# Filter transposed in 16 bits, other first loads, an uneven last tile, and a new fixed order, in a kernel of a long convolution beside a token-mixing MLP

## The chip, the cores and the metric

The kernel runs on one core of a Trainium2 chip. The time is the device time of one execution in microseconds; the median of three runs before the change is 177.09 us (176.99 to 177.10). A core has five engines that each work through a queue of their own in order: TensorE (PE, the matmuls; PEld is its weight load), VectorE (DVE), ScalarE (ACT), GpSimd (POOL) and SyncE (SP, which here only starts transfers). TensorE writes into PSUM, from which another engine has to move every result into the main on-chip memory (an *evacuation*).

## What is computed

```python
x = A_q                                                # 2048 tokens x 640 channels, bf16
g = sigmoid((x * gate_w).sum(-1, keepdims=True))
# a: a gated long convolution
k_shift[t] = sum_j A_k[t - 3 + j] * shift_k[j]         # four taps, causal
kv = k_shift * A_v
y  = irfft(rfft(kv, 4096) * rfft(ssm_k, 4096))[:2048]  # one filter of 2048 taps for each channel
a  = q * (y + kv * ssm_D)
# b: a MLP that mixes tokens
h  = layernorm(x)                                      # over the 640 channels
u  = gelu(einsum("bsd,sf->bdf", h, w1) + b1)           # 2048 tokens -> 1536
b  = transpose(einsum("bdf,fs->bds", u, w2) + b2)      # 1536 -> 2048 tokens
out = g * a + (1 - g) * b
```

## The kernel before

Everything is matmuls on 128x128 blocks. The Fourier transforms are products with cosine and sine tables: FE and FN, which are made on the chip with a sine on ScalarE, and FO, which is loaded. The program writes the whole computation as 649 operations (a matmul group, a step on another engine, or a transfer), each with a number. Three strings fix what runs when:

- `_ORDER` (L1318) lists the numbers. Each engine's queue, SP's queue of transfers included, gets its operations in this order.
- `_SLOTS` gives each matmul group one of four PSUM slots (128 x 1024 in f32, two banks each). A group waits until its slot has been evacuated.
- `_ENG` says for the operations that either engine can do ("A" ScalarE, "D" VectorE) which one does: the evacuations of the filter part, the normalizations of the layer norm, and the permutations of k.

Waits follow from the regions that operations read and write (class `_Tracker`; its `mm`, L286 to L309, issues every matmul, at L298; every ScalarE step of a general kind is at L600, VectorE's and POOL's elementwise steps at L556 and L570, and the evacuations at L615 for ScalarE and L616 for VectorE).

The parts that the change touches:

- *Filter.* `ssm` holds the filters, five blocks `db` of 128 channels, in two halves `h` of 1024 taps. `transp(h, db)` (L798) transposes one half of one block with eight matmuls against the identity (group "wtr") and evacuates the slot, 128 x 1024, to `wT` with a factor 1/1024. For h = 0 a POOL step first adds the skip term D, which lies in `dcol`, to the first tap; `dcol` is an evacuation of the transposed small rows `rows` (group "cst"). `wblock(h, db)` (L818) multiplies `wT` with the tables in two groups of 16 matmuls ("W") and evacuates each ("Wb"). Ten transpositions, 80 matmuls; twenty W groups, 320 matmuls.
- *k and kv.* POOL forms four `KF`, the short convolution's taps on diagonals, from `cw` (L971). A tile of k is permuted (`k_turn`, L702, "kperm"), transposed by a transfer into KT, and multiplied with KF on TensorE; the product with v is transformed.
- *Layer norm.* `ln_tile` (statistics, VectorE), `ln_scale` (POOL) and `ln_apply` ("nrm", either engine), for 16 rows of 640.
- *MLP.* The first product in groups of eight matmuls of 320 columns, with the Gelu as evacuation into GT; ScalarE has to load another function table between the sine and the first Gelu. b1 goes through a transposition of its own (`consts`, L791) into `cc`. The second product (L1108 to L1125) takes the 640 columns of a tile as 320 + 320 in two banks. The last tile (hk = 3) has its two halves one after the other, so that the first half is complete early.
- *End.* The inverse transforms, and for each tile the combination with g. In the last tile two VectorE steps ("fin", `last_stt`, L624), one for each column half, take PSUM and the convolution's part together, and one store of 160 KB follows.

In the order before, SP starts its first loads as: the X tile 2, filter block 1, the first half of block 0, block 2, FO in two parts, X3, b1, block 3, X1, three quarters of X0, k, block 4, k, the last quarter of X0, the second half of block 0, w1. TensorE begins with dummy matmuls on zeros (`zz`), a pair of which stands later between two transpositions. POOL adds D to block 1 and block 0, then to block 2, then makes two KF, and so on. ScalarE's table load for the Gelu comes just before the first Gelu.

Of the kernel before, what the change touches and what calls it, by code (L numbers as in the profile page):

```python
# [19 lines left out]
class _Tracker:  # L20
# [265 lines left out]
    def mm(self, ps_ap, lhsT, rhs, start, stop, final_val, inc, transpose=False):  # L286
        acc_r = []
        for a in (lhsT, rhs):
            for r in self.regions(a):
                acc_r.append((r, "R"))  # L290
        acc = list(acc_r)
        ps_regs = self.regions(ps_ap)
        if start:
            for r in ps_regs:
                acc.append((r, "W"))
        need = self.deps_for("PE", acc)
        self.do_waits("PE", need)
        ins = self.nc.tensor.matmul(ps_ap, lhsT=lhsT, rhs=rhs, start=start, stop=stop, skip_group_check=True)  # L298
        src = ("eng", "PE", final_val)
        for reg, mode in acc_r:  # L300
            self.add_record(reg, "R", src)
        for r in ps_regs:
            self.add_record(r, "W", src)
        if inc:
            ins.then_inc(self.clk["PE"], 1)
            self.cnt["PE"] += 1
            assert self.cnt["PE"] == final_val, (self.cnt["PE"], final_val)
            self.hist["PE"].append(dict(self.known["PE"]))
        return ins  # L309
# [123 lines left out]
def _build(nc, A_q, A_k, A_v, A_shift_k, A_ssm_k, A_ssm_D, B_x, B_w1, B_b1, B_w2, B_b2, gate_w, out):  # L433
# [10 lines left out]
    with ExitStack() as es:  # L444
# [190 lines left out]
        def memset(eng, ap, val, prio=None):  # L635
            return nolock(eng, 0.2, lambda s: T.op(eng, lambda e: e.memset(ap, val), [], [ap]), [], [ap], prio=prio)

        def mms(vt, items, prio=None, name="mm"):
            dur = sum(max(n_of(r) / 2400.0 + 0.0025, 0.056) for _, _, r, _, _ in items)
            rd = []  # L640
            for _, l, r, _, _ in items:
                rd += [l, r]

            def emit(s):
                fv = T.cnt["PE"] + 1
                for k_, (o, l, r, st, sp) in enumerate(items):
                    T.mm(o(s), l, r, st, sp, fv, k_ == len(items) - 1)
            return SC.add("PE", dur, emit, rd, [], prio=prio, vt=vt, name=name)

        ndma = [0]  # L650
# [16 lines left out]
        def dr(t, off, ap):  # L667
            return bass.AP(tensor=t.tensor, offset=t.offset + off, ap=ap)
# [10 lines left out]
        def ssm_load(h, a, b):  # L679
            dma(ssm[:, a:b, 1024 * h:1024 * h + 1024], dr(A_ssm_k, 128 * S * a + 1024 * h, [[S, 128], [128 * S, b - a], [1, 1024]]), 128 * (b - a) * 2048, chain=True, rate=({0: 262.0, 1: 223.0}.get(a, RL3)) if h == 0 else 385.0)  # L680
# [9 lines left out]
        def qrow(hk):  # L690
            return row8(A_q, hk) if hk >= 2 else dr(A_q, 512 * hk * D, [[4 * D, 128], [1, 4 * D]])

        def x_load(hk):
            dma(X[:, hk, :, :], qrow(hk), 128 * 5120, chain=True, rate=(352.0 if hk == 0 else 415.0))

# [24 lines left out]

        small(rows[0:ND, 0, 128:256], dr(A_ssm_D, 0, [[128, ND], [1, 128]]), 1280, "QA")
        small(rows[0:20, 0, 0:128], dr(A_shift_k, 0, [[128, 20], [1, 128]]), 5120, "QA")
        ssm_load(0, 0, 1)
        for a, b in ((0, 1), (1, 4)):
            dma(X[:, 0, a:b, :], dr(A_q, a * D, [[4 * D, 128], [1, (b - a) * D]]), 128 * 1280 * (b - a), chain=True)
        ssm_load(1, 0, 1)
        for db in range(1, ND):
            dma(ssm[:, db, :], dr(A_ssm_k, 128 * S * db, [[S, 128], [1, S]]), 128 * 4096, chain=True)
        for p in range(2):
            dma(FO[:, p, :, :, :, :].rearrange("q a b c d -> q (a b c d)"), dr(odd_tab, 1024 * p, [[2048, 128], [1, 1024]]), 128 * 2048, chain=True)  # L730
        for hk in range(1, 4):
            x_load(hk)
        small(bt[:, 0:8].rearrange("q (a b) -> q a b", a=2), dr(B_b2, 0, [[4, 128], [512, 2], [1, 4]]), 2048, "SP", chain=True)
        small(bt[:, 8:16], dr(B_b2, 1024, [[8, 128], [1, 8]]), 2048, "SP", chain=True)
# [63 lines left out]
        def transp(h, db):  # L798
            vt = _VT("cv")
            items = []  # L800
            if h == 0:
                w0 = V(ssm, db * S, [[1, 1]])
                tt("POOL", w0, w0, dcol[:, db:db + 1], ALU.add)
            for j in range(7, -1, -1):
                items.append(((lambda s, j=j: s[:, 128 * j:128 * j + 128]), V(ssm, db * S + 1024 * h + j, [[8, 128]]), ident[:, :], True, True))
            m_ = mms(vt, items, name="wtr")
            evac("wT", V(wT, 2 * h * SL + 128 * db, [[SL, 2], [D, 4], [1, 128]]), (lambda s: s[:, :].rearrange("q (a b c) -> q a b c", a=2, b=4)), vt, 1.0 / 1024.0)

        def table(p, kt, c, k2):
            if p % 2:  # L810
# [291 lines left out]
        def w2t(hk, p, ft):  # L1102
            if hk < 2:
                return V(W2, (W2S[hk][ft // 4] + ft % 4) * 512 + p, [[4, 128]])
            return V(W2, W2P[ft] * 512 + 4 * (hk - 2) + p, [[8, 128]])

        INVP = ((0, 2, 1, 3), (1, 3, 0, 2))
        for hk, p in [(hk, p) for hk in range(2) for p in range(4)] + [(hk, p) for p in INVP[1] for hk in (2, 3)]:  # L1108
            for a in {(1, 0): (4, 6, 8), (2, INVP[1][0]): (10,)}.get((hk, p), ()):
# [6 lines left out]
            for a in range(na):  # L1116
                items = []
                for ft, ci in order[a * (24 // na):(a + 1) * (24 // na)]:
                    items.append((chk(ci), w2t(hk, p, ft), GT[:, ft, 320 * ci:320 * ci + 320], ft == 0, ft == FT - 1))
                mms(vt, items, name="m2")  # L1120
                if last_:
                    vt.keep = True
                    lastvt.append(vt)
# [111 lines left out]
        def inverse(h, Z, G=None):  # L1235
            for p in INVP[h]:
# [25 lines left out]
                if h == 1 and p == INVP[1][-1]:  # L1262
# [2 lines left out]
                    t = 12 + p  # L1265
                    ts("DVE", cg[:, 1, :], cg[:, 1, :], c2[:, t:t + 1], None, ALU.add, mode=2)
                    for ci in range(2):
                        last_stt(O1[:, 3, p, 320 * ci:320 * ci + 320], chk(ci), omg[:, t:t + 1], cg[:, 1, 320 * ci:320 * ci + 320], lastvt[ci])
                    dma(rows_of(1, p, 1, 1), O1[:, 3, p, :], 128 * 1280, sem="out")
                elif h == 0:  # L1270
                    dma(ov, qv, 128 * 2560, stream="POOL", prio=0, accum=True)
                    dma(rows_of(0, p, 0, 2), ov, 256 * 1280, sem="out")
# [43 lines left out]


_ORDER = """  # L1318
# [22 lines left out]
"""  # L1341
_ENG = "DAAAAADDAAAAAADDDDDAAADDDADDDDADDAAAAAAAAAAAAAAADD"
_SLOTS = "1120021323201331122022011133001030332021001010110220110131230121002123231321103301332230032032101133201012203121332133113300113"
# [1 line left out]
_INS = ['A_q', 'A_k', 'A_v', 'A_shift_k', 'A_ssm_k', 'A_ssm_D', 'B_x', 'B_w1', 'B_b1', 'B_w2', 'B_b2', 'gate_w']  # L1345
_OUTS = [((1, 2048, 640), 'bfloat16')]
# [23 lines left out]
```

## Time and profile before

| | before |
|---|---|
| median of 3 runs | 177.09 us (176.99 to 177.10) |
| profiled execution | 177.12 us, of which the span from the first to the last instruction is 175.1 us |
| granted TensorE clock | 1.00 throughout |
| TensorE busy | 170.0 us (97%) |
| VectorE busy | 168.9 us (96%) |
| ScalarE busy | 107.6 us (61%) |
| POOL busy | 42.7 us (24%) |
| data moved | 44.06 MB in 33248 packets, mean 252 GB/s |

The busy time of each engine over five stretches (us, busy time, number of instructions, granted clock, share of the transfer engines, GB/s):

```profile
core 0: us, PE busy (x) PEld busy (x) DVE busy (x) ACT busy (x) POOL busy (x), PEclk, DMA share, GB/s
0.00:6.60 6.60, 5.25 (x20) 1.78 (x21) 4.73 (x19) 2.79 (x4) 1.62 (x12) 1.00 0.73 227
6.60:30.30 23.70, 23.70 (x404) 23.40 (x405) 23.45 (x62) 22.56 (x26) 17.80 (x31) 1.00 1.09 332
30.30:44.30 14.00, 13.48 (x152) 10.32 (x149) 13.87 (x14) 12.69 (x16) 0.00 (x0) 1.00 1.10 326
44.30:171.90 127.60, 127.59 (x988) 102.72 (x988) 125.80 (x94) 69.56 (x116) 23.24 (x19) 1.00 0.93 230
171.90:175.10 3.20, 0.00 (x0) 0.00 (x0) 1.01 (x2) 0.00 (x0) 0.00 (x0) 1.00 0.76 266
```

The first stretch ends with the first transposition of the filter; the second holds the whole filter part; the third the k part and the first half of the MLP's first product up to the first Gelu; the fourth everything else up to the last matmul; the fifth the closing steps and the last store. A row of the timeline is start, length, engine, line, instruction, output <- inputs with shapes, and in brackets the idle time ahead of it with what ended it. Matmuls are pipelined, and the end that a row gives is modelled.

### The profile page before, as it was taken

The page shows a single profiled execution, that of the slowest core. Times are in us where ns is not written, and L with a number is a line of the kernel's source. Part 1 is how long each engine was busy: PE and PEld are TensorE (multiplying, and loading weights), DVE is VectorE, ACT ScalarE, POOL GpSimd, SP SyncE. Part 2 cuts the span into 40 slices and gives each one's busy share as a digit, 9 for nine tenths or more (in the row PEclk, how much of TensorE's full clock was granted, in tenths as well). Part 3 has the DMA queues.
Part 4 walks back from the last instruction along what each step waited for, and adds up shares of the span by engine and source line. Part 5 has one row for each costly group of instructions (what it writes and reads, how often), then busy time and mean ns, then how long its engine had stood idle before and what let it go on. Part 6 is the DMA issues. An engine that isn't in the chain of part 4 may idle for free.

```text
span 175.1 us, 3683 instructions
## 1 busy us (share of the span) xinstructions
PE 170.0 (97%) x1559; PEld 138.2 (79%) x1559; DVE 168.9 (96%) x187; ACT 107.6 (61%) x160; POOL 42.7 (24%) x62
## 2 busy tenths in 40 slices
PE   7999999999899999999999999999999999999992
PEld 2599999877697767777777778888899998698782
DVE  7899999999999999999999999999999999999984
ACT  4499999997999997877556214222215105645760
POOL 3199891000000650003202202220055000052200
PEclk9999999999999999999999999999999999999999
DMA  5999999999999799992999999999939999549598
GB/s 144 397 421 405 376 200 225 380 375 221 179 383 356 172 192 192 186 358 57 178 174 365 353 211 349 282 207 240 300 108 187 197 177 372 241 65 209 106 233 292
DMA packets 33248, 44.06 MB, mean 252 GB/s; under 512 B 12112, under 2 KB 24656, under 8 KB 33104
## 3 DMA queue, kind: packets, MB, share of 16 engines
q1 hardware_dynamic: 28024, 32.68, 57.6%
q0 software_dynamic: 5168, 11.14, 37.4%
q8 instruction: 12, 0.20, 0.4%
q14 instruction: 4, 0.03, 0.1%
q10 hardware_dynamic: 40, 0.01, 0.0%
HBM read 27.44 MB, written 2.62 MB: 172 GB/s over the span
## 4 chain that ended last, share of the span: by engine, by line
PE 93%; DMA 3%; ACT 2%; DVE 0%; DVEq 0%; SPq 0%; issue 0%
PE pp L298 93%; DMA ssm<-in_A_ssm_k_dram 3%; ACT L600 1%; ACT ksh L600 1%; ACT GT L600 0%; DVE O L627 0%; DVEq L426 0%; SPq L272 0%
## 5 line engine op out<-in xcount | busy, mean ns | idle before, releaser
L298 PE MATMUL pp<-X,ring 128*128 128x320 bf16 x384 | 55.4, 299 | 0.5 <-ACT GT L600 0.5
L556 DVE TENSOR_TENSOR C<-C 128x2560 bf16<-128x2560 bf16 (+2 forms) x38 | 54.6, 1485 | 0.3 <-ACT C L600 0.2
L298 PE MATMUL pp<-GT,W 128*128 128x320 bf16 x384 | 53.6, 299 | 0.0
L298 PEld LDWEIGHTS pp<-GT,W 128*128 128x128 bf16 x384 | 48.0, 129 | 4.6
L298 PEld LDWEIGHTS pp<-X,ring 128*128 128x128 bf16 x384 | 37.0, 98 | 15.0 <-ACT GT L600 0.8
L600 ACT ACTIVATE O<-pp,c,omg 128x640 bf16<-128x640 f32 x15 | 12.9, 883 | 24.8 <-PE pp L298 24.8
L267 POOL DMA_DIRECT2D C<-C x8 | 10.5, 1674 | 51.1 <-DVE C L556 30.0
L600 ACT ACTIVATE C<-pp 128x640 bf16<-128x640 f32 x32 | 20.4, 711 | 2.0 <-PE pp L298 2.0
L600 ACT ACTIVATE cgb<-pp,gg 128x640 bf16<-128x640 f32 x16 | 12.1, 795 | 13.3 <-PE pp L298 7.6
L615 ACT ACTIVATE C<-pp 128x1024 bf16<-128x1024 f32 x18 | 17.1, 1051 | 0.3 <-PE pp L298 0.3
L600 ACT ACTIVATE gq<-gq 128x640 bf16<-128x640 bf16 x16 | 11.6, 727 | 5.7 <-DVE gq L556 5.7
L556 DVE TENSOR_TENSOR tm<-C,C 128x5120 bf16<-128x5120 bf16 x5 | 14.1, 2819 | 0.1
L897 DVE BATCH_NORM_STATS2 stats<-X 128x6 f32<-128x320 bf16 x32 | 13.1, 470 | 0.4 <-DMA X<-in_A_q_dram 0.2
L298 PE MATMUL pp<-wT,FO 128*128 128x128 bf16 x160 | 12.4, 219 | 0.0
L600 ACT ACTIVATE GT<-pp,cc 128x640 bf16<-128x640 f32 x12 | 9.3, 793 | 4.8 <-PE pp L298 4.7
L298 PE MATMUL pp<-C,GTB 128*128 128x320 bf16 x80 | 11.9, 299 | 0.0
L298 PE MATMUL pp<-wT,FE 128*128 128x128 bf16 x120 | 11.7, 219 | 0.0
L556 DVE TENSOR_TENSOR SS<-C 128x2560 bf16<-128x2560 bf16 x8 | 11.7, 1482 | 0.0
L267 POOL DMA_DIRECT2D O<-q_hi x4 | 4.8, 1324 | 27.7 <-DVE q_hi L556 27.7
L600 ACT ACTIVATE ksh<-pp 128x1024 bf16<-128x1024 f32 (+1 forms) x12 | 10.1, 908 | 1.4 <-PE pp L298 1.3
L267 POOL DMA_DIRECT2D C<-q_hi x4 | 4.8, 1198 | 23.8 <-DVE q_hi L556 10.9
L556 DVE TENSOR_TENSOR C<-tm 128x2560 bf16<-128x2560 bf16 x7 | 10.3, 1487 | 0.1
(92 smaller groups left out, 225.3 us busy)
## 6 DMA issues: line engine op xcount, KB each, us to landing
ring<-in_B_w_dram SPq DMA_DIRECT2D x12, 512.0 KB, 8.8
W<-in_B_w_dram SPq DMA_DIRECT2D x12, 512.0 KB, 6.8
C<-C POOLq DMA_DIRECT2D x8, 640.0 KB, 8.8
kn<-in_A_k_dram SPq DMA_DIRECT2D x4, 640.0 KB, 9.6
C<-q_hi POOLq DMA_DIRECT2D x4, 640.0 KB, 9.7
out_dram<-O SPq DMA_DIRECT2D x7, 320.0 KB, 3.2
ssm<-in_A_ssm_k_dram SPq DMA_DIRECT2D x4, 512.0 KB, 7.0
X<-in_A_q_dram SPq DMA_DIRECT2D x3, 640.0 KB, 7.3
```

What stands on the lines that cost most here:

```text
L267: ins = engobj.dma_start(out_ap, in_ap, accum_op=ALU.add, max_dma_last_dim=2560)
L298: ins = self.nc.tensor.matmul(ps_ap, lhsT=lhsT, rhs=rhs, start=start, stop=stop, skip_group_check=True)
L556: o_ = SC.add(eng, d, lambda s: T.op(eng, lambda e: e.tensor_tensor(o, a, b, op), rd, [o]), rd, [o], prio=prio, name="tt")
L600: return T.op("ACT", lambda e: e.activation(o, src, func, **kw), rr + [src], ww)
L615: return either(name, o, i, [], lambda e, src: e.activation(o, src, ACT.Copy, **kw), lambda e, src: e.tensor_copy(o, src) if scale == 1.0 ...
L897: ops.append(SC.add("DVE", 0.38, (lambda o, i: lambda s: T.op("DVE", lambda e: e.bn_stats(o, i), [i], [o]))(o, i), [i], [o]))
```

## The change

1. `mm` passes its flag `transpose` on. The filter's transpositions are issued as transpositions proper, which write 16-bit results into PSUM: a group then fills half a slot, one bank in place of two, and its evacuation reads 128 x 1024 of bf16 in place of f32.
2. `_ENG`: four of the ten evacuations to `wT` are VectorE's (block 3's first half; the second halves of blocks 2, 3 and 4), in place of two others (the first halves of blocks 0 and 2). Two "Wb" evacuations go from VectorE to ScalarE. Of the 16 normalizations VectorE does 12 in place of 11. One more permutation of k (tile 2) goes to ScalarE: VectorE keeps three.
3. Loads: block 1 of the filter comes in two halves, and block 0 whole. X tile 2 comes as one quarter and three quarters (`xpart`), and X0 whole.
4. The last tile of the MLP's second product takes its columns as 512 + 128. The two closing steps have these widths, and each has a store of its own (128 KB and 32 KB). That makes 650 operations.
5. `_ORDER` and `_SLOTS` are new. The first loads go out as: X3, b1, block 2, block 1 in halves, X2 in two pieces, block 0, FO in two parts, X0, block 4, X1, k, block 3, k, w1. ScalarE's table load for the Gelu comes right after the sine, ahead of `dcol`, `cc` and `cw`. b1 is transposed ahead of the filter. TensorE transposes block 2 (second half), block 1 (first half), block 2 (first half), then after a pair of dummies block 1 (second half), and W groups follow. POOL adds D to blocks 2 and 1, makes three KF, and then adds D to block 0. At the end, the closing step of the 128 columns and its store come before that of the 512.

```diff
-        ins = self.nc.tensor.matmul(ps_ap, lhsT=lhsT, rhs=rhs, start=start, stop=stop, skip_group_check=True)
+        ins = self.nc.tensor.matmul(ps_ap, lhsT=lhsT, rhs=rhs, start=start, stop=stop, skip_group_check=True, **({"is_transpose": True} if transpose else {}))
...
-        def mms(vt, items, prio=None, name="mm"):
+        def mms(vt, items, prio=None, name="mm", transpose=False):
...
-                    T.mm(o(s), l, r, st, sp, fv, k_ == len(items) - 1)
+                    T.mm(o(s), l, r, st, sp, fv, k_ == len(items) - 1, transpose)
...
+        def xpart(hk, a, b):
+            t = qrow(hk)
+            return bass.AP(tensor=t.tensor, offset=t.offset + a * D, ap=[list(t.ap[0]), [1, (b - a) * D]])
...
-        ssm_load(0, 0, 1)
+        ssm_load(0, 1, 2)
         for a, b in ((0, 1), (1, 4)):
-            dma(X[:, 0, a:b, :], dr(A_q, a * D, [[4 * D, 128], [1, (b - a) * D]]), 128 * 1280 * (b - a), chain=True)
-        ssm_load(1, 0, 1)
-        for db in range(1, ND):
+            dma(X[:, 2, a:b, :], xpart(2, a, b), 128 * 1280 * (b - a), chain=True)
+        ssm_load(1, 1, 2)
+        for db in [d for d in range(ND) if d != 1]:
...
-        for hk in range(1, 4):
+        for hk in [k for k in range(4) if k != 2]:
...
-                items.append(((lambda s, j=j: s[:, 128 * j:128 * j + 128]), V(ssm, db * S + 1024 * h + j, [[8, 128]]), ident[:, :], True, True))
-            m_ = mms(vt, items, name="wtr")
-            evac("wT", V(wT, 2 * h * SL + 128 * db, [[SL, 2], [D, 4], [1, 128]]), (lambda s: s[:, :].rearrange("q (a b c) -> q a b c", a=2, b=4)), vt, 1.0 / 1024.0)
+                items.append(((lambda s, j=j: s[:, 64 * j:64 * j + 64].bitcast(BF16)), V(ssm, db * S + 1024 * h + j, [[8, 128]]), ident[:, :], True, True))
+            m_ = mms(vt, items, name="wtr", transpose=True)
+            evac("wT", V(wT, 2 * h * SL + 128 * db, [[SL, 2], [D, 4], [1, 128]]), (lambda s: s[:, 0:512].bitcast(BF16).rearrange("q (a b c) -> q a b c", a=2, b=4)), vt, 1.0 / 1024.0)
...
+        LASTC = (0, 512, 640)
...
-                    items.append((chk(ci), w2t(hk, p, ft), GT[:, ft, 320 * ci:320 * ci + 320], ft == 0, ft == FT - 1))
+                    c0, c1 = LASTC[ci:ci + 2] if last_ else (320 * ci, 320 * ci + 320)
+                    items.append(((lambda s, ci=ci, n=c1 - c0: s[:, 512 * ci:512 * ci + n]), w2t(hk, p, ft), GT[:, ft, c0:c1], ft == 0, ft == FT - 1))
...
-                        last_stt(O1[:, 3, p, 320 * ci:320 * ci + 320], chk(ci), omg[:, t:t + 1], cg[:, 1, 320 * ci:320 * ci + 320], lastvt[ci])
-                    dma(rows_of(1, p, 1, 1), O1[:, 3, p, :], 128 * 1280, sem="out")
+                        c0, c1 = LASTC[ci:ci + 2]
+                        last_stt(O1[:, 3, p, c0:c1], (lambda s, ci=ci, n=c1 - c0: s[:, 512 * ci:512 * ci + n]), omg[:, t:t + 1], cg[:, 1, c0:c1], lastvt[ci])
+                        o_ = rows_of(1, p, 1, 1)
+                        dma(bass.AP(tensor=o_.tensor, offset=o_.offset + c0, ap=[list(o_.ap[0]), [1, c1 - c0]]), O1[:, 3, p, c0:c1], 128 * 2 * (c1 - c0), sem="out")
...
 (_ORDER, _ENG and _SLOTS: all three strings are new)
```

More of the change, by code (lines that the diff above doesn't have):

```diff
@@ L1318 @@
 _ORDER = """
[22 rows of a table removed]
-"""
-_ENG = "DAAAAADDAAAAAADDDDDAAADDDADDDDADDAAAAAAAAAAAAAAADD"
-_SLOTS = "1120021323201331122022011133001030332021001010110220110131230121002123231321103301332230032032101133201012203121332133113300113"
[22 rows of a table added]
+"""
+_ENG = "AAAAAAAAADAAAAADDDDADDDDDDAADDADDAAAAAADAADAADAAAD"
+_SLOTS = "1211230021121032302130333220100200132011110003002200313302032022013013320221200231313321021023113013201123002101030022130211312"
 _INS = ['A_q', 'A_k', 'A_v', 'A_shift_k', 'A_ssm_k', 'A_ssm_D', 'B_x', 'B_w1', 'B_b1', 'B_w2', 'B_b2', 'gate_w']
```

44 rows, old and new, of the table _ORDER are left out of this document.

## The prediction

> **What bounds the kernel now.** I read three views. First the page: its engine shares and its chain of waits by line.
>
> ```profile
> PE 170.0 (97%) x1559; PEld 138.2 (79%) x1559; DVE 168.9 (96%) x187; ACT 107.6 (61%) x160; POOL 42.7 (24%) x62
> ...
> PE pp L298 93%; DMA ssm<-in_A_ssm_k_dram 3%; ACT L600 1%; ACT ksh L600 1%; ACT GT L600 0%; DVE O L627 0%; DVEq L426 0%; SPq L272 0%
> ```
>
> VectorE is nearly as busy as TensorE, but 93% of the chain is matmuls (one helper, L298, issues them all). So a microsecond counts only if it lies in front of a matmul, before 6.60 us or after 171.90 us. Second, the same chain in order of time (start, length, what):
>
> ```profile
> 1.19 5.37 DMA ssm<-in_A_ssm_k_dram
> ...
> 6.60 27.17 PE pp L298 x443
> ...
> 33.78 7.29 PE pp L298 x88
> ...
> 41.09 1.02 ACT ksh L600
> ...
> 42.13 1.28 ACT L600
> ...
> 43.43 0.81 ACT GT L600
> ...
> 44.28 127.63 PE pp L298 x988
> ...
> 171.93 0.55 DVE O L627
> 172.48 0.46 DVEq L426
> ```
>
> TensorE starts on the filter's first landing, loses one stretch to three ScalarE instructions in a row, then runs 127.6 us to the end. Third, the timeline (start, length, engine, instruction, idle before it), for what the chain calls continuous:
>
> ```profile
> 6.60 1.21 PE L298 MATMUL pp<-ident,ssm 128*128 128x128 bf16 x16 [0.18 <-DMA ssm<-in_A_ssm_k_dram]
> 7.65 0.59 PE L298 MATMUL pp<-zz 128*128 128x512 bf16 x2
> 8.08 1.69 PE L298 MATMUL pp<-ident,ssm 128*128 128x128 bf16 x24
> 8.74 4.09 POOL L556 TENSOR_TENSOR KF<-cw,m 128x1120 bf16<-128x1120 bf16 x2
> 9.60 0.33 PE L298 MATMUL pp<-wT,FE 128*128 128x128 bf16 x3
> 14.07 0.65 PE L298 MATMUL pp<-ident,ssm 128*128 128x128 bf16 x8
> 14.76 0.34 PE L298 MATMUL pp<-wT,FE 128*128 128x128 bf16 x3
> 32.52 1.25 PE L298 MATMUL pp<-X,ring 128*128 128x320 bf16 x8
> 42.13 1.28 ACT L600 ACT_TABLE_LOAD   x1
> 42.52 1.25 PE L298 MATMUL pp<-X,ring 128*128 128x320 bf16 x8
> 44.28 0.99 PE L298 MATMUL pp<-X,ring 128*128 128x320 bf16 x6 [0.51 <-ACT GT L600]
> ```
>
> A matmul's modelled end overlaps its successor, so a loss is read from start to start. Back to back, starts are 55.9 ns apart for 128 columns, 135.9 ns for 320 and 215.9 ns for 512. Eight of 320 from 42.52 last to 43.61, the next starts at 44.28: 0.67 us lost. From 32.52 likewise: 33.61 against 33.78, 0.17. Eight of 128 from 14.07 last to 14.52, the next block starts at 14.76 (a 12-column transposition of b1 lies between): 0.24. From 6.60 to 9.60, 40 transpositions need 2.24 us and the two dummy matmuls (zz) 0.43, which leaves 0.33. All gaps after 6.60 come to about 1.45 us: that, plus what precedes and follows the matmuls, is all that an order can win.
>
> **Part 1: 16-bit transposition.** Eighty matmuls of 128 columns stay eighty of 128. Their price as transpositions is in no row. Ends: 42.6 ns (the 96-column matmuls' pitch) and 111 ns (twice 55.9, since the dummies before 5.4 us start every 0.43 us and later ones every 0.216). I take 55.9, the row of the same shape: 0 us; the ends are −1.1 and +4.4 us (80 times the difference). [...]
>
> **Part 2: evacuations.** The lines of VectorE by shape:
>
> ```profile
> L616 DVE TENSOR_SCALAR wT<-pp 128x1024 bf16<-128x1024 f32 x2 | 2.4, 1182 | 0.0
> L570 DVE TENSOR_SCALAR pint<-pint 128x1024 int16<-128x1024 int16 x1 | 0.4, 428 | 0.0
> L556 DVE TENSOR_TENSOR pint<-tb,jrow 128x1024 int16<-128x1024 int16 x1 | 0.7, 692 | 0.0
> ```
>
> The fourth price, 16-bit from PSUM, lies between 428 ns and 1182 ns; I take 692, the 16-bit row at the middle rate. [...] VectorE then has 4 × 0.69 + 12 × 0.43 + 3 × 0.81 = 10.4 us of the movable work, against 2 × 1.18 + 2 × 1.22 + 11 × 0.43 + 4 × 0.81 = 12.8: 2.4 us less. ScalarE keeps 26 evacuations of 1024, loses one normalization (0.98) and gains one permutation of 2560 (about 2.3, from 0.73 at 640 and 1.15 at 1024). Both lie beside TensorE; VectorE's 2.4 us are slack and count nothing. The permuted tile's transposing DMA stays on SP's queue. If VectorE's cover is gone, the evacuation of block 4's second half decides: it is VectorE's now and queues behind a permutation that waits for k. It holds the PSUM slot of a following filter block: +0.15 us (0 to 0.3; with 1182 ns, 0.5 to 0.9 for all such waits).
>
> **Part 3: the order.** (a) The Gelu table's load moves from 42.13 to behind the sine, before dcol: the 0.67 us go. Next behind it is ksh (41.09 to 42.11): the Gelu step can then end at 42.94, 0.67 us before TensorE is free at 43.61. (b) b1 is transposed before the filter lands: −0.24. b1's 3 KB transfer comes second on SP's queue; at its old place, the neighbours landed 1.27 us apart against 1.26 to 1.32 elsewhere: 0. (c) 33.6: −0.17. The 0.10 us at 51.1 and 0.05 at 150.9 I leave as they are.
> (d) New: dcol waits for the table. The sine comes at about 4.4 (0.8 later, behind another VectorE step) and takes 1.15, the load 1.28 to 6.84, dcol to about 7.13. POOL adds the D row to two filter blocks, 0.20 each, to 7.53, and the second transposition starts at 7.56 rather than 7.05: 0.51 against the 0.33 of that stretch now, +0.2. Behind dcol on ScalarE wait cw, which KF needs, and the first evacuations; both are counted in this. (e) New: POOL forms three KF (2.03 each, two in 4.09) before it adds to block 0: 7.56 + 6.1 + 0.2 = 13.86, where TensorE, counted through its new order from 7.56, would be free at 13.5: +0.33. Behind KF also wait the small layer-norm steps (0.24 each) for normalizations that VectorE does only after 23 us now. (f) A slot of the kv transform waits for ScalarE: +0.13.
> (g) Loads: SP issues one about every 0.44 us, the link then takes about 405 KB/us. First come X3 (5.30, as the first X tile now), b1, block 2 (6.56), block 1 in halves (7.2, 7.8), X2 in two pieces, block 0, the two FO (11.4, 12.05). By the new order FO is used from 11.9 and 12.4: hidden by 0.35 us; it costs what it is late. Transfers of k move by under 1.5 us, behind VectorE's queue.
>
> **Part 4: last tile.** 12 × 215.9 + 12 × 55.9 = 3.26 us equals 24 × 135.9. Both closing VectorE steps still follow the last matmul: 640 columns and two starts as before, 0.55 and 0.46 us. The last store is 128 KB, not 160: 32/405 = −0.08; its 0.35 us issue is behind the 32 KB store's, which goes out half a us earlier: I take −0.06 (−0.08 to +0.4, one more issue in its way).
>
> **Sum.** −0.67 − 0.24 − 0.17 + 0.20 + 0.33 + 0.15 + 0.13 − 0.06 = −0.33 us. From the profiled execution, 177.12 us (175.1 of span and 2.0 around it), 176.79; the median of the runs shown, 177.09, stands 0.03 below it: 176.8.
>
> **Rivals.** (A) The new waits (d to f and the slot, 0.81 us) don't come, because dcol or the POOL order is quicker than by my rows: −1.14, 176.0. For it: each is a difference of two nearly equal times. (B) Ends on the other side: VectorE's 16-bit evacuation stays at 1182 ns, so the four cost 2.0 us more just where the slots are tight, and TensorE waits 0.5 to 0.9 rather than 0.15: 177.2 to 177.6. It decides from 0.68 us of waits on. Against it: the 428 and 692 ns rows. (C) Slower at the start: the chain sine, table, dcol, POOL is longer than (d) has it; each 0.1 us of it is 0.1 us of TensorE's, so half a us gives 177.3. For it: four engines take turns in it, none with room. [...] (E) The 16-bit form gains nothing because VectorE's time is hidden: that is the sum already.
>
> **Numbers.** The sum's case, 176.4 to 177.2, has 0.46, half of it beyond 0.2% (0.35 us, about what a measurement can tell from no change): 0.23 faster, 0.23 same. A has 0.22, faster. B 0.15, of which 0.02 same. C 0.11. D 0.06. So faster 0.45, same 0.25, slower 0.30. For 8 in 10 the range drops D and the far end of A and C: 176.0 to 177.9.
>
> **What would show it.** Right: the table load before dcol and no gap before the first Gelu (a); the second transposition at about 7.5 (d); a gap near 13.5 ended by POOL (e); four wT evacuations on VectorE of about 0.69 us (B: 1.18); transposition starts 55.9 ns apart (D: more); last matmul near 171.6. Wrong: dummies or matmuls at twice their pitch after 6.6 us, FO or k later than TensorE asks, or gaps ended by ScalarE between 15 and 30 us, where 26 evacuations of 1.05 us leave it little room.

## The result and the profile after

The change made the kernel slower: 178.75 us (median of four runs, 178.66 to 179.20) against 177.04 us before; the ratio is 1.0102, with a 95% interval of 1.0084 to 1.0120. The profiled execution took 178.66 us, of which the span is 176.9 us (before 175.1). So 1.8 us have to be found. The page's first lines, shares of the engines and the chain by line:

```profile
PE 169.6 (96%) x1558; PEld 137.4 (78%) x1559; DVE 167.1 (94%) x187; ACT 108.9 (62%) x160; POOL 42.7 (24%) x62
...
PE pp L298 78%; DMA ring<-in_B_w_dram 6%; ACT C L615 4%; DMA ssm<-in_A_ssm_k_dram 3%; ACT wT L615 3%; SPq L272 2%; ACT cgb L600 1%; ACT GT L600 1%; ACT C L600 0%; DVEq L426 0%; DVE O L627 0%; SPq L265 0%
```

Before, 93% of the chain was matmuls. Now 78% is, and a transfer that the chain before did not contain stands second: `ring`, a part of W1. The same chain in order of time (start, length, what):

```profile
2.06 5.68 DMA ssm<-in_A_ssm_k_dram
...
7.78 0.72 PE pp L298 x8
...
8.53 2.85 ACT wT L615 x3
...
15.96 3.68 ACT C L615 x4
...
19.68 24.51 PE pp L298 x346
...
48.99 9.96 DMA ring<-in_B_w_dram
...
58.99 109.28 PE pp L298 x808
...
173.80 0.35 DVE O L627
```

The three ScalarE pieces of before, with the table load between 42 and 43.4 us, are gone. In their place there are three new stretches: a filter transfer that lands at 7.74, ScalarE evacuating without a break from 8.53 to 19.64, and a W1 transfer that lands at 58.94. The timeline shows what each costs TensorE (start, length, instruction, idle before it):

```profile
6.14 0.71 PE L298 MATMUL pp<-ident,ssm 128*128 128x128 bf16 x8 [0.27 <-DMA ssm<-in_A_ssm_k_dram]
7.78 1.18 PE L298 MATMUL pp<-ident,ssm 128*128 128x128 bf16 x16 [0.94 <-DMA ssm<-in_A_ssm_k_dram]
8.80 0.59 PE L298 MATMUL pp<-zz 128*128 128x512 bf16 x2
9.24 0.66 PE L298 MATMUL pp<-ident,ssm 128*128 128x128 bf16 x8
9.73 0.33 PE L298 MATMUL pp<-wT,FE 128*128 128x128 bf16 x3
...
19.68 0.34 PE L298 MATMUL pp<-wT,FE 128*128 128x128 bf16 x3
...
58.99 1.26 PE L298 MATMUL pp<-X,ring 128*128 128x320 bf16 x8 [1.47 <-DMA ring<-in_B_w_dram]
```

Read from start to start, as in the prediction, TensorE lost 1.10 us ahead of 7.78, 0.31 ahead of 19.68, 0.24 at 54.4 and 1.63 ahead of 58.99. Before, its larger losses were 0.20 at 14.5, 0.17 at 33.6, 0.67 at 43.5 and 0.10 at 51.1. That is 3.28 against 1.14, or 2.14 more; the first transposition starts 0.46 earlier (6.14 against 6.60). The difference, 1.7 us, is the change in time. The 0.46 is mostly scatter between two executions, not a merit of the new order: in the four kernels below that keep the first loads of before and b1's old place, the first transposition started at 6.17 to 6.28. (A further 0.22 us that the trace seems to show ahead of 170.48 is one missing record of a 512-column matmul; back to back these start 0.216 apart.)

### The profile page after: what moved, and what is told of

Read it like the earlier page. It is cut to its first block, busy times and chain, and to the rows that moved or that the text cites. A ratio compares the mean times of both kernels' runs of the same rounds, so it can differ in the third digit from the quotient of the medians.

```text
span 176.9 us, 3673 instructions
## 1 busy us (share of the span) xinstructions
PE 169.6 (96%) x1558; PEld 137.4 (78%) x1559; DVE 167.1 (94%) x187; ACT 108.9 (62%) x160; POOL 42.7 (24%) x62
## 4 chain that ended last, share of the span: by engine, by line
PE 78%; DMA 9%; ACT 9%; SPq 2%; issue 0%; DVEq 0%; DVE 0%
PE pp L298 78%; DMA ring<-in_B_w_dram 6%; ACT C L615 4%; DMA ssm<-in_A_ssm_k_dram 3%; ACT wT L615 3%; SPq L272 2%; ACT cgb L600 1%; ACT GT L600 1%; ACT C L600 0%; DVEq L426 0%; DVE O L627 0%; SPq L265 0%
## 5 line engine op out<-in xcount | busy, mean ns | idle before, releaser
L556 DVE TENSOR_TENSOR C<-C 128x2560 bf16<-128x2560 bf16 (+2 forms) x38 | 55.2, 1486 | 0.5
L298 PE MATMUL pp<-GT,W 128*128 128x320 bf16 (+2 forms) x383 | 52.8, 299 | 0.1
L298 PEld LDWEIGHTS pp<-GT,W 128*128 128x128 bf16 x384 | 47.2, 129 | 5.4
L267 POOL DMA_DIRECT2D C<-C x8 | 11.4, 1728 | 51.9 <-DVE C L556 49.0
L615 ACT ACTIVATE C<-pp 128x1024 bf16<-128x1024 f32 x20 | 19.3, 1102 | 0.0
L901 DVE BATCH_NORM_STATS2 stats<-X 128x6 f32<-128x320 bf16 x32 | 13.8, 472 | 1.9 <-DMA X<-in_A_q_dram 1.9
L298 PE MATMUL pp<-C,GTB 128*128 128x320 bf16 x80 | 11.4, 299 | 0.0
L298 PEld LDWEIGHTS pp<-C,GTB 128*128 128x128 bf16 x80 | 7.7, 98 | 3.0 <-ACT cgb L600 0.2
```

Source lines behind the costliest of these rows:

```text
L267: ins = engobj.dma_start(out_ap, in_ap, accum_op=ALU.add, max_dma_last_dim=2560)
L556: o_ = SC.add(eng, d, lambda s: T.op(eng, lambda e: e.tensor_tensor(o, a, b, op), rd, [o]), rd, [o], prio=prio, name="tt")
L615: return either(name, o, i, [], lambda e, src: e.activation(o, src, ACT.Copy, **kw), lambda e, src: e.tensor_copy(o, src) if scale == 1.0 ...
L901: ops.append(SC.add("DVE", 0.38, (lambda o, i: lambda s: T.op("DVE", lambda e: e.bn_stats(o, i), [i], [o]))(o, i), [i], [o]))
```

## The experiments

The kernel before ran beside each group of these, 17 to 29 times: its medians were 176.9 to 177.1 us, its single runs 176.6 to 178.6. Single runs of the kernels below scatter by up to 2 us as well, so differences of less than some 0.3 us between medians are not read; what decides there is the trace.

**The W1 part that came late.** On SP's queue, behind the two transposing transfers of k, the order of before was: W1 part 1 of the second chunk (operation 244), v, v, the parts 247, 246 and 245, and the gate weights (47). The changed order is 245, v, v, gate weights, 244, 247, 246, and the matmuls at 57.3 us need 244. Two edits of the changed kernel's order:

```diff
-... 245 ... 239 ... 238 47 ... 244 ... 247 ... 246 ...
+... 245 ... 239 ... 238 ... 244 ... 247 ... 246 47 ...
```

> The changed kernel with one transfer moved on SP's queue: the gate weights (128 rows of 1280 B) go out behind the four parts of W1's second chunk, as before the change, not ahead of three of them. Theory 1 (load order): in the changed kernel they took 1.37 us between their neighbours' landings (56.11 to 57.48 us) and TensorE waited for the part that landed at 58.94. That part now lands at about 57.6, TensorE's gap at 57.3 shrinks from 1.63 to about 0.25 us, and the time is 178.75 - 1.4 = 177.4. Rival (the kv stage is bound by ScalarE and VectorE, which are 97 to 100% busy there): TensorE only waits at the next place, the gain is under 0.7 us, and the time is above 178.0.

```diff
-... 245 ... 239 ... 238 47 ... 244 ... 247 ... 246 ...
+... 244 245 ... 239 ... 238 ... 247 ... 246 47 ...
```

> As the one before, and the part of W1's second chunk that TensorE needs first also goes out first, ahead of another part and two v tiles. Theory 1: it lands at about 53, TensorE has no gap at 57.3, and the time is 178.75 - 1.63 = 177.1. The v tiles land some 1.5 us later, at about 56.0 and 57.6; VectorE multiplies with them at about 57.5, so up to 0.2 us may come back there. Rival as above: over 178.0.

Measured: 177.84 us (ratio to before 1.0045, 1.0024 to 1.0067) and 177.49 us (1.0024, 1.0003 to 1.0045). The timelines around 58 us, of the first and of the second:

```profile
58.18 1.26 PE L298 MATMUL pp<-X,ring 128*128 128x320 bf16 x8 [0.53 <-DMA ring<-in_B_w_dram]
```

```profile
56.98 0.95 PE L298 MATMUL pp<-KF,KT 128*128 128x128 bf16 x16
57.84 1.25 PE L298 MATMUL pp<-X,ring 128*128 128x320 bf16 x8
```

With the gate weights last, the part landed at 58.13 and the loss fell from 1.63 to 0.69 us; the time fell by 0.9. With the part first, it landed at 52.53, the loss was 0.07 and the time 1.26 us lower. So the theory holds and the rival (ScalarE and VectorE would keep the time above 178.0) falls; the gains were 0.5 and 0.4 us smaller than expected. In the first run one reason shows: the part ahead, 245, already came 0.4 us later than in the changed kernel (53.34 against 52.95).

**b1's transfer.** The late filter transfer stands behind the 3 KB of b1, which the change moved from the eighth to the second place on SP's queue. Two experiments: the changed kernel without that transfer, and the kernel before with only that transfer moved up.

```diff
-        small(rows[0:12, 2, 0:128], dr(B_b1, 0, [[128, 12], [1, 128]]), 3072, "SP", chain=True)
...
-            items.append(((lambda s: s[:, 0:12]), rows[0:12, 2, 0:128], ident[0:12, 0:12], True, True))
+            items.append(((lambda s: s[:, 0:12]), rows[0:12, 0, 0:128], ident[0:12, 0:12], True, True))
```

> The changed kernel without the 3 KB transfer of b1, which goes out second on SP's queue; b1's transposition takes 12 rows of the short convolution's taps in its place, so b1 is left out of the result. Theory 2 (the small early transfer holds one transfer engine back): the first half of filter block 1 lands near 6.8 instead of 7.74 us, TensorE's gap at 6.6 shrinks from 1.10 to about 0.5 (POOL's addition at 7.17 is then the limit), and the time is 178.75 - 0.6 = 178.15. Rival (the lateness comes from the halves or from chance): it lands at about 7.3 to 7.7, the later start of every transfer being the only thing gone, and the time is 178.5 to 178.8.

In the order of the kernel before:

```diff
-... 13 ... 6 ... 2 ... 7 ... 10 11 ... 14 ... 17 ... 8 ...
+... 13 17 ... 6 ... 2 ... 7 ... 10 11 ... 14 ... 8 ...
```

> The kernel before with another step of the change alone: the 3 KB transfer of b1 goes out second on SP's queue instead of eighth. Theory 2 (it holds back what is behind it): filter block 1 lands 0.7 to 1.1 us later than at 6.56 us, so do the transfers behind it, TensorE's first transposition moves with it, and the time is 177.7 to 178.1; more where TensorE falls to half rate in the longer wait, as it did in the run with plain transpositions (107 ns from start to start after 1.8 us of idling). Rival (the halves of block 1 or chance were late): landings move by no more than 0.1 us and the time stays at 177.0.

Measured: 178.19 us, 0.56 below the changed kernel; and 178.12 us, 1.04 above the kernel before (ratio 1.0057, 1.0042 to 1.0071). Without b1, the landings behind block 2 (5.99) were block 1's halves at 6.70 and 7.39 and X2 at 7.83 and 9.04; with it 7.74, 8.40, 8.85 and 10.05 behind 6.09. In the kernel before with b1 early, block 1 still came at 6.11, but what follows at 8.32 and 9.58, against 7.21 and 8.53. In the four other traces with these first loads and b1 in its old place, these three landed at 6.13 to 6.23, 6.78 to 6.92 and 8.25 to 8.63. TensorE's timeline in the run with b1 early:

```profile
6.42 1.16 PE L298 MATMUL pp<-ident,ssm 128*128 128x128 bf16 x16
7.42 0.59 PE L298 MATMUL pp<-zz 128*128 128x512 bf16 x2
8.36 0.71 PE L298 MATMUL pp<-ident,ssm 128*128 128x128 bf16 x8 [0.35 <-DMA ssm<-in_A_ssm_k_dram]
9.63 0.58 PE L298 MATMUL pp<-ident,ssm 128*128 128x128 bf16 x6 [0.56 <-DMA ssm<-in_A_ssm_k_dram]
```

And in the changed kernel without b1:

```profile
6.04 1.36 PE L298 MATMUL pp<-ident,ssm 128*128 128x128 bf16 x15
7.56 0.78 PE L298 MATMUL pp<-ident,ssm 128*128 128x128 bf16 x9 [0.17 <-POOL ssm L556]
```

There TensorE lost 0.18 us ahead of its second group and 0.33 ahead of that group's last matmul, which waits for POOL's addition, in place of 1.10.

So 3 KB in twelve rows of 256 B, put near the head of the queue, made everything from the next transfer but one onward about 1.0 us late, in two different orders, and the kernel before became 1.04 us slower. The other traces bear it out: in the five with b1 second, the third large transfer lands 2.9 to 3.6 us after the first, in the nine others 1.9 to 2.7. That is shown; by what mechanism is not, nor that one transfer engine is held back, as theory 2 put it. It isn't the packets' own time, which is at most 18 ns each in the traces before and after the change.

**Plain transpositions.** The changed kernel with the transpositions undone:

```diff
-                items.append(((lambda s, j=j: s[:, 64 * j:64 * j + 64].bitcast(BF16)), V(ssm, db * S + 1024 * h + j, [[8, 128]]), ident[:, :], True, True))
-            m_ = mms(vt, items, name="wtr", transpose=True)
+                items.append(((lambda s, j=j: s[:, 128 * j:128 * j + 128]), V(ssm, db * S + 1024 * h + j, [[8, 128]]), ident[:, :], True, True))
+            m_ = mms(vt, items, name="wtr")
```

> The changed kernel with the transpositions undone: ordinary matmuls into 32-bit PSUM again, everything else as changed. Theory (the form of the transposition isn't what costs): transposition starts are 55.9 ns apart either way; VectorE's four evacuations take 1.18 instead of 0.66 us, and as VectorE is not what the gaps wait for, the time is 178.75 to 179.2. Rival (transpositions proper are dearer or let the clock fall): the time falls below 178.4.

Measured: 179.21 us (ratio 1.0120, 1.0088 to 1.0152): the expected end of the range. The traced execution (179.49 us) shows something that was not expected:

```profile
5.84 0.18 PE L298 MATMUL pp<-ident,rows 12*128 12x12 bf16 x1
7.64 2.73 PE L298 MATMUL pp<-ident,ssm 128*128 128x128 bf16 x24 [1.62 <-DMA ssm<-in_A_ssm_k_dram]
10.17 1.06 PE L298 MATMUL pp<-zz 128*128 128x512 bf16 x2
11.02 0.73 PE L298 MATMUL pp<-ident,ssm 128*128 128x128 bf16 x8
11.59 0.33 PE L298 MATMUL pp<-wT,FE 128*128 128x128 bf16 x3
```

In this execution already the first filter block came late (7.59, against 6.1 to 6.3 in the other four with b1 second), TensorE idled 1.62 us, and then ran at half rate: the granted clock was 0.50 from 7.78 to 11.20 us, 24 transpositions from 7.64 to 10.17 are 105 ns apart, the dummies 0.43 us. In the changed kernel the idle time was 0.94 us, and the 16 transpositions from 7.78 to 8.80 are 64 ns apart, the dummies 0.22 us. The plain transpositions of the kernel before start 66 ns apart, so the half rate followed the idle time, not the kind of matmul. TensorE was 1.9 us behind the changed kernel at the first filter product (11.59 against 9.73), yet its span is only 0.6 us longer (177.4 against 176.9): at 59.6 its wait for the W1 part had shrunk to 0.07 us, for that part came at 59.09, nearly as ever. The W1 part hid the loss. The other three executions, with a granted clock of 1.00, took 179.04 to 179.30 us, so the half rate is not what puts this median 0.46 us above the changed kernel's, and single runs of the changed kernel reach 179.20. This run therefore can't price the form of the transposition; one of the next does.

**The good parts alone, on the kernel before.** The early table load (operation 38 right behind 36 on ScalarE), the 16-bit transpositions (the matmul flag, the bank half and the evacuation as in the change, nothing else), and both:

```diff
-36 ... 405 38 371 ...
+36 38 ... 405 371 ...
```

> The kernel before with one step of the change alone: the load of the Gelu's table comes right behind the sine. Theory (that load on ScalarE was the chain at 41 to 44 us): TensorE's 0.67 us gap at 43.5 goes, the first transpositions wait at most 0.1 us more for dcol, and the time is 177.04 - 0.6 = 176.4. Rival (ScalarE or VectorE stand right behind it in the kv stage): the gap comes back further on, and the time is 176.9 to 177.1.

```diff
-            m_ = mms(vt, items, name="wtr")
+            m_ = mms(vt, items, name="wtr", transpose=True)
```

> The kernel before with the 16-bit transpositions alone (which engine evacuates what, loads and order as before). Theory (parts 1 and 2 of the prediction): starts stay 55.9 ns apart, VectorE's two evacuations of that kind take 0.66 instead of 1.18 us, ScalarE's stay at 1.05, and as VectorE's time isn't on the chain the time stays at 177.0 within 0.2. [...]

> The kernel before with the early table load and the 16-bit transpositions together, to see whether the two good parts alone beat both kernels. Theory: the gap at 43.5 is gone, VectorE has 1.0 us more slack, and the time is as with the table load alone, 176.2 to 176.7. Rival: one of the two brings back a wait, 177.0 or more.

Measured: the table load 176.69 us (ratio 0.9985, 0.9959 to 1.0011, single runs 176.15 to 178.09), the transpositions 177.02 us (0.9993, 0.9973 to 1.0014), both 176.65 us (0.9967, 0.9944 to 0.9991). In the first of them the gap at 43.5 is gone, as a line of its chain shows, and the profiled execution took 176.19 us, but the interval includes no change.

```profile
33.56 137.45 PE pp L298 x1096
```

The second is the theory's result: the time stays, VectorE's evacuation is cheaper, ScalarE's is not.

```profile
L615 ACT ACTIVATE wT<-pp 128x1024 bf16<-128x1024 bf16 x8 | 8.1, 1043 | 1.3 <-PE pp L298 1.3
...
L616 DVE TENSOR_SCALAR wT<-pp 128x1024 bf16<-128x1024 bf16 x2 | 1.3, 666 | 0.6 <-PE pp L298 0.6
```

The third beats both kernels: 0.33% below the kernel before, and its chain is almost nothing but matmuls:

```profile
PE pp L298 98%; DVE O L627 0%; DVEq L426 0%; DVE zz L636 0%
```

**What else the new order holds.** With the W1 part first and the gate weights last, b1 was also moved: its transfer behind X0, its transposition between two kv groups (below, the queues of SP, TensorE and ScalarE; `_SLOTS` differs in one place).

```diff
-14 ... 17 7 2 5 3 4 6 10 11 12 9 ...   95 ... 209 68 75 ...   96 50 69 ...
+14 ... 7 2 5 3 4 6 10 11 12 17 9 ...   390 ... 95 264 ...     258 ... 96 265 ...
```

> The changed kernel with W1's needed part first and the gate weights last, as in the run before on that, and b1 moved: its transfer behind X0, its transposition between two kv groups at about 42.7 us, its evacuation behind one of theirs. Theories 1 and 2 together: no gap at 57.3, block 1 lands at 6.7, TensorE's gaps before 8 us shrink from 1.1 to about 0.5, and the time is 177.49 - 0.6 to 0.9 = 176.6 to 176.9, under the kernel before. Rival (TensorE only waits for ScalarE's evacuations from 8 to 20 us instead): 177.3 or more.

Then dcol and cw ahead of the table load:

```diff
-36 38 ... 49 ... 50 ...
+36 ... 49 ... 50 38 ...
```

> As the one before, and ScalarE evacuates dcol and cw ahead of the table load instead of behind it. Theory (term d of the prediction): dcol is done at about 5.7 instead of 7.0 us, the additions wait for the landings alone, 0.3 us of TensorE's gap near 7.2 go, and the time is 0.3 below the run before on this list, 176.3 to 176.6. Rival (the evacuations on ScalarE set the pace from 8 to 20 us, so an earlier start is lost again): no difference.

Measured: 177.16 us (0.9992, 0.9975 to 1.0010) and 177.31 us (1.0014, 1.0003 to 1.0024). The first gained 0.33 us, not 0.6 to 0.9; the second nothing: the rivals were right. Part of the first miss is scatter: block 1 landed at 7.34 there and at 7.04 in the second, where 6.7 was expected from the run without b1. The rest is that two waits further on swallow an earlier start. One is ScalarE's evacuations, as the rivals have it. The other shows in the run with the W1 part first. Its timeline, of VectorE and then of TensorE:

```profile
18.39 1.28 DVE L901 BATCH_NORM_STATS2 stats<-X 128x6 f32<-128x320 bf16 x3 [1.04 <-DMA X<-in_A_q_dram]
...
20.16 0.78 DVE L710 COPY kp<-kn 128x2560 bf16<-128x2560 bf16 x1
20.84 0.69 DVE L616 TENSOR_SCALAR wT<-pp 128x1024 bf16<-128x1024 bf16 x1
...
21.59 0.34 PE L298 MATMUL pp<-wT,FE 128*128 128x128 bf16 x3 [0.22 <-DVE wT L616]
```

VectorE waits for X1, then does statistics, the permutation of k and only then the evacuation of block 4's second half, whose PSUM slot the next filter group needs. That group starts 3.23 us after X1 lands: 18.36 and 21.59 here, 17.54 and 20.77 with dcol first, 17.52 and 20.74 without b1. TensorE can be ready earlier; it will not go on earlier. One last edit gave one of ScalarE's evacuations (202, at 16.9 us) to VectorE:

```diff
-... 117(D) 202(A) ...
+... 202(D) 117(D) ...
```

> The run with dcol first, and one of ScalarE's evacuations of the filter stage (second half of block 0, at 16.9 us) given to VectorE, which idles there from 16.6 to 17.6 us waiting for X1. Theory 3 (in the new order ScalarE's evacuations, 0.91 us apart without a break from 8 to 20 us, set TensorE's pace): TensorE's gaps of 0.31 and 0.32 us at 18.6 and 20.4 go or shrink to 0.1, and the time is 177.31 - 0.5 = 176.8. Rival (the gaps come from something else, or come back in the k and kv stages): no change, 177.2 to 177.4.

Measured: 177.10 us (0.9990, 0.9970 to 1.0010), 0.2 below. The waits for ScalarE went, the one for VectorE grew; TensorE's timeline:

```profile
20.91 0.34 PE L298 MATMUL pp<-wT,FE 128*128 128x128 bf16 x3 [0.68 <-DVE wT L616]
```

From start to start 0.84 us are lost here, where the two gaps before this edit were 0.31 and 0.32. Theory 3 names the right cause of the gap at 18.6, but the second gap was VectorE's, and the gain stopped there. With all of these edits the new order is level with the old one, not ahead of it.

**The last tile.** To the two good parts on the kernel before, the last tile as 512 and 128 columns was added:

```diff
-... 626 647 646 648
+... 626 648 646 649 647
```

> The kernel before with three steps of the change: the early table load, the 16-bit transpositions, and the last tile as 512 and 128 columns with a store each. Theory (term of the last tile): from the start of the two closing steps to the last landing 2.76 us as in the changed kernel, instead of 2.86 before, so the time is 0.1 below the run with the two parts, 176.5 to 176.6, within what can be told; it stays below the kernel before. Rival: the second store's issue comes late and the end is 0.3 us later, 176.9 or more.

Measured: 177.53 us (1.0027, 1.0005 to 1.0049), a miss by 0.9. Its profiled execution took 176.18 us with the span of the run without this step, 174.2, but nine of its twelve runs took 177.15 to 178.73. The traced one shows no loss at the end, and no gain: from the start of the closing steps to the last landing it took 2.86 us (171.02 to 173.88), against 2.84 in the run without this step (171.04 to 173.88). What the other executions waited for isn't in a trace, and whether the uneven tile is to blame stays open.

## Why the prediction was wrong

The forecast was 176.8 us, 176.0 to 177.9; it was 178.75. The reading of before held: only what lies in front of a matmul counts. Step by step:

- *Part 1, 0 us for the transpositions*: right. The 16-bit form alone left the time at 177.02. In the changed kernel they start 60 to 64 ns apart (66 for the plain ones of the kernel before, from 6.60 to 7.65), and no half rate followed them: the granted clock was 1.00 from 5.4 to 20 us. As single instructions, the first after a pause lasted 276 to 277 ns (at 6.14 and 7.78 us) and most others 223 to 226, but they overlap: what counts is the distance of their starts. Rival D, which had 0.06 in the forecast, was that transpositions are dearer or let the clock fall; no run shows that of the 16-bit form, and with 177.02 us for this step alone it falls.
- *Part 2, 692 ns for VectorE's evacuation*: it took 668 and 666 ns, 3 to 4% less than the row that was taken. Rival B falls with it: the four cost no more time than said. That the saving is slack was right too. (By the sum, rival B makes the kernel 0.35 us slower from 0.83 us of waits on; the 0.68 in its text is what has to come on top of the 0.15.)
- *(a), −0.67*: right. No gap at 43.5, in the changed kernel and with this step alone.
- *(b)*: the gap of the b1 transposition went, but "b1's 3 KB transfer comes second on SP's queue; at its old place, the neighbours landed 1.27 us apart against 1.26 to 1.32 elsewhere: 0" is the first step that failed. The price was read at the eighth place of the queue, and the transfer was moved to the second. There it makes what follows 1.0 us late; at the eleventh, in the runs with b1 moved back, its neighbours landed 1.28 to 1.29 us apart again.
- *(d), +0.20*: the wait came where it was put, but it was 1.10 us long and dcol was not its cause: dcol was done at 7.0, the first addition ran at 7.17, and block 1 landed at 7.74. The stretch from the first transposition to the first product lost 1.37 us (3.59, less 32 transpositions and the dummies) instead of 0.53; the start 0.46 us earlier gave part of it back.
- *(e), +0.33*: mis-sized; it cost 0.04. POOL's addition for block 0 ran from 14.03 to 14.22, as forecast within 0.4 us, but the group started at 13.85: the added tap is read by the last of its eight matmuls alone. That can be read in the loop that counts j down from 7 to 0.
- *The slot of block 4's second half, +0.15*: 0.03 in the changed kernel, for ScalarE's queue had already cost 0.31 at 19.3, and 0.84 where that was mended. The place was right; the evacuations of ScalarE, named only as a sign of error, were the term that was missing.
- *The kv slot, +0.13*: 0.24, at 54.4.
- *(g)*: FO came at 12.01 and 12.68, 0.6 us later than forecast, through b1, and cost 0.05. Of the later transfers the prediction said only: "Transfers of k move by under 1.5 us, behind VectorE's queue." This is the second step that failed, and the dearest: W1's second chunk, v and the gate weights changed places behind the k transfers, and no term looked at them. (The loads of k moved by more, too: the third landed at 34.23 against 32.04.) The rows of before would have warned, but not given the size. There the first part landed at 51.76, the two v 1.52 and 1.65 later, the next W1 part 1.50, and the gate weights, last, 0.41. In the new order these add up to 56.8 for part 244, only half a us ahead of 57.3, where TensorE wanted it. It came at 58.94, because the part that goes first landed 1.19 us later (52.95; the transposing transfer of k ahead of it was 0.82 later) and because the gate weights, no longer last, took 1.37 in place of 0.41.
- *Part 4, −0.06*: −0.10 in the profile of the changed kernel, from the start of the closing steps to the last landing (173.80 to 176.56 us, against 171.93 to 174.79 before). But in the trace of the run that adds this step to the two good parts the stretch was no shorter (2.86 against 2.84), so the −0.10 is not shown to come from the uneven tile, and its agreement with −0.06 may be luck; as the median of that run was a miss, this term is not settled.

With the measured sizes: −0.67 − 0.20 − 0.17 − 0.10 for what went, 1.37 − 0.33 − 0.46 = +0.58 at the start, + 0.04 + 0.31 + 0.24 + 1.63 for the waits, and −0.10 for the tail give +1.56; 1.71 were measured between the medians, and 1.8 between the spans. Both failed steps are transfers, 2.7 us between them (1.63, and 1.37 against 0.33), less what the earlier start gave back. The rival on the start (C) had the place of the first, but put it down to engines taking turns; none of the rivals had a transfer as its mechanism.

## What to carry to other kernels

Where a new order of transfers comes with a change, list for each consumer what now stands ahead of its transfer on the queue and add up landing distances from the trace; TensorE's order alone does not show it. Where that leaves little room, count it as a likely wait. A transfer's price holds at the place where it was read: a few rows of 256 B cost nothing at the eighth place of the queue and 1.0 us at the second, the gate weights 0.41 us at the end and 1.37 ahead of others. Waits that end with a landing (X1, W1) swallowed what was gained ahead of them, so test a gain together with the wait behind it, and test the parts of a mixed change alone: here two of them together beat both kernels.

## What the runs showed of the hardware that was not expected

- 3 KB in twelve rows, second on the queue, made the transfers from the next but one on 1.0 us late (7.74 against 6.70 us; 8.32 against 7.21); in one execution already the next (7.59 against 6.1 to 6.3).
- The gate weights, 160 KB that read one row of 1280 B for all 128 partitions, took 1.37 us from the landing before to their own, nearly as long as the 512 KB of W1 behind them (1.46). That holds for their place ahead of W1's parts (1.37 to 1.74 us in three traces); behind them they took 0.38 to 1.05 us in the eleven others.
- After 1.62 us without work TensorE ran at half rate in the one execution that shows it (granted clock 0.50 from 7.78 to 11.20 us, 105 ns for 128 columns); after 0.94 us, in the changed kernel, it did not (granted clock 1.00, 64 ns).
- ScalarE evacuated 128 x 1024 in the same time from 16 and from 32 bits (1043 and 1042 ns); VectorE took 666 against 1182.
